# The second layer's products by Strassen's seven-product scheme on blocks of 1024 tokens

## The chip, the cores and the metric

The kernel runs on one core of a Trainium2 chip. TensorE (PE) multiplies matrices from SBUF into PSUM, VectorE (DVE) and ScalarE (ACT) work elementwise, SyncE (SP) issues DMAs between DRAM and SBUF; GpSimd (POOL) is all but unused here. The metric is the device time of one execution in microseconds (us), median of several runs. Each engine executes its own instructions in a fixed order, and waits by semaphores for the others.

## The reference

Chunked attention with memory keys, then two feed-forward layers without bias, on 3072 tokens of width 512, all in float32:

```python
# attention: 4 batches, 8 heads, 768 positions, width 64; chunks of 32 see 8 memory keys + 56 neighbours
x = attention(q, k, v, mem_k, mem_v).transpose(0, 2, 1, 3).reshape(3072, 512)
h = x @ w_in                                   # layer one: 512 x 2048
g = np.maximum(h, 0.0) + np.log1p(np.exp(-np.abs(h)))
y = g @ w_out                                  # 2048 x 512
h2 = y @ w2_in                                 # layer two: 512 x 2048
out = (h2 - np.tanh(h2)) @ w2_out              # 2048 x 512
```

## The kernel before

**Precision.** TensorE multiplies operands of a shorter float (F32R). Every float32 operand is therefore kept as a high and a low part, and a product is three matmuls: high by high, high by low, low by high (`mm3`, lines 285 to 287 of before). Weights arrive as 64-bit floats, are rebuilt as float32 (`split_w`, lines 127 to 131) and split into the two parts (138, 140).

**Work.** The 3072 tokens go in six blocks of 512 (`j`). For each block and each of 16 slices of the hidden width (`f`), `ff_h` makes 128 hidden features x 512 tokens (4 slices of the width, so 12 matmuls of 128x128 by 128x512) in one of two PSUM banks `ps_h`; `chain1` (layer one) or `chain2` (layer two) applies the nonlinearity and splits the result into `gh`, `gl`; two `f` later (`LAG`), `run_y` adds its share to four output banks `ps_y`, 12 matmuls more. So a block is 16 x 24 = 384 matmuls in either layer, and layer two is 6 x 384 = 2304. In layer two `ff_y2` takes `gh`, `gl` as the stationary side, so its result is token-major and leaves by `out2`. Between the layers `out1` splits each result bank (354, 355) and stores it to DRAM (`x2d`), and `load_x2` brings a block of it back.

**Attention** runs for the first block in an opening whose order is written out by hand (`OPENING`), about the first 120 us; afterwards, during block `j` of layer one, for block `j+1`: a unit of 128 tokens at a time, in pieces between the matmuls (`at_do`): scores (line 186), softmax (DVE 206, 210, 223 to 226, ACT 220), transposes (231) two `f` after the scores, values (250), and the split into `x` (262, 264).

**Order.** PE's order is that of the code. The other engines' order is made by a list scheduler before the run, which takes what is ready, the urgent first: `hp(HPC)` lifts the chains, `hp(HPA)` attention, and `hp(HPW)` puts the splitting of layer two's weights last; it takes place in layer one's last block and layer two's first one. At run time each engine, SP's queue of DMA issues too, goes strictly in that order, and whoever waits holds up what is behind. Tiles come from pools with a fixed number of buffers (`gpool` 3, `opool` 4), and a new tile waits until an old one's last reader, or the DMA that stores it, is done.

Of the kernel before, what the change touches and what calls it, by code (L numbers as in the profile page):

```python
# [8 lines left out]
F32 = mybir.dt.float32  # L9
# [11 lines left out]
P = 128  # L21
# [38 lines left out]
HPA = 60  # L60
HPW = -80
EXP_BIAS = 2.0 ** -112
# [3 lines left out]
def attention_ffn_ffn(  # L66
# [18 lines left out]
    opool = ctx.enter_context(tc.tile_pool(name="o", bufs=4))  # L85
    apool = ctx.enter_context(tc.tile_pool(name="a", bufs=2))
    dpool = ctx.enter_context(tc.tile_pool(name="d", bufs=1, space=bass.MemoryType.DRAM))
# [34 lines left out]
    def split_w(raw, f, kinds="io", t=None):  # L122
        n = len(kinds)
        lo, hi = raw[:, :, :, 0], raw[:, :, :, 1]
        c = opool.tile([P, n, 512], U32, name="o")
        w = c.bitcast(F32)
        nc.scalar.mul(w, hi.bitcast(F32), EXP_BIAS)
        yield
        nc.vector.tensor_scalar(out=c, in0=c, scalar1=3, scalar2=None, op0=ALU.logical_shift_left)  # L129
        for src, k, op in ((hi, 0x80000000, ALU.bitwise_and), (lo, 29, ALU.logical_shift_right)):  # L130
            nc.vector.scalar_tensor_tensor(  # L131
                out=c, in0=src, scalar=k, in1=c, op0=op, op1=ALU.bitwise_or
            )
        yield
        if t is None:
            t = wpool.tile([P, n, 2, 512], F32R, name=f"w{f}")
        h, l = t[:, :, 0, :], t[:, :, 1, :]
        nc.scalar.copy(out=h, in_=w)
        yield
        nc.vector.tensor_tensor(out=l, in0=w, in1=h.bitcast(F32), op=ALU.subtract)  # L140
        for i, kind in enumerate(kinds):
            weights[kind, f] = h[:, i], l[:, i]

    def run(steps):
# [138 lines left out]

    def mm3(ps, ah, al, bh, bl, first, last):
        nc.tensor.matmul(out=ps, lhsT=ah, rhs=bh, start=first, stop=False)  # L285
        nc.tensor.matmul(out=ps, lhsT=ah, rhs=bl, start=False, stop=False)  # L286
        nc.tensor.matmul(out=ps, lhsT=al, rhs=bh, start=False, stop=last)  # L287

# [29 lines left out]

    def chain2(key, ps):
        t = tpool.tile([P, N], F32, name="t")  # L320
        nc.scalar.activation(out=t, in_=ps, func=AF.Tanh)  # L321
        nc.vector.tensor_tensor(out=t, in0=ps, in1=t, op=ALU.subtract)  # L322
        run(split_g(key, t, nc.vector))

    def split_g(key, t, hi_eng):
# [16 lines left out]

    def ff_y2(key, f):
        gh, gl = gt.pop(key)
        wh, wl = weights["o", f]
        for e in range(UB):
            c = slice(e * P, (e + 1) * P)
            mm3(ps_y[e], gh[:, c], gl[:, c], wh, wl, f == 0, f == NF - 1)

    def out1(j):  # L350
        for e in range(KT):
            o = opool.tile([P, 2, N], F32R, name="o")
            src = ps_y[e][:, :N]
            nc.scalar.copy(out=o[:, 0, :], in_=src)
            nc.vector.tensor_tensor(
                out=o[:, 1, :], in0=src, in1=o[:, 0, :].bitcast(F32), op=ALU.subtract
            )
            nc.sync.dma_start(out=x2d[j][:, e], in_=o.bitcast(F32))

    def out2(j):  # L360
        for e in range(UB):
            t0 = j * N + e * P
            o = opool.tile([P, DM], F32, name="o")
            if t0 == NTOK - P:
                nc.vector.tensor_copy(out=o[:, : DM // 2], in_=ps_y[e][:, : DM // 2])
                nc.scalar.copy(out=o[:, DM // 2 :], in_=ps_y[e][:, DM // 2 :])
            elif e % 2:
                nc.vector.tensor_copy(out=o, in_=ps_y[e])
            else:
                nc.scalar.copy(out=o, in_=ps_y[e])  # L370
            nc.sync.dma_start(out=out[t0 : t0 + P, :], in_=o)

    def load_x2(j):
        x = x_tile(NB + j)
        nc.sync.dma_start(out=x.bitcast(F32), in_=x2d[j])

    class Weights:
# [6 lines left out]

        def run(self, count):
            while self.at < min(count, NF):
                self.load(self.at + 1)
                run(split_w(*self.staged.pop(0)))
                self.at += 1

    nc.scalar.preload_act_table_set("natural_log_exp_and_others")
    nc.vector.memset(zeros, 0.0)
    make_identity(nc, ident)

    w1, w2 = Weights(w1i, w1o), Weights(w2i, w2o)

# [3 lines left out]
    def run_y():  # L400
        layer, j, f = pend.pop(0)
        if layer == 1:
            ff_y1((1, j, f), f)
            if f == NF - 1:
                with hp(HPC):
                    out1(j)
        else:
            ff_y2((2, j, f), f)
            if f == NF - 1:
                with hp(HPC):  # L410
                    out2(j)

    with tc.manual_schedule(engines={mybir.EngineType.PE}):
# [68 lines left out]

        pend = [(1, 0, NF - LAG + i) for i in range(LAG)]
        for j in range(1, NB):
# [18 lines left out]
            for f in range(NF):  # L503
                ps = ff_h(f, slot, x)
                with hp(HPC):
                    run(chain1((1, j, f), ps, nc.vector))
                piece(2 * f)
                pend.append((1, j, f))
                if len(pend) > LAG:
                    run_y()  # L510
                piece(2 * f + 1)
                slot += 1
                if j == NB - 1 and f >= LAG:
                    with hp(HPW):
                        w2.load(f - LAG + 1)
                        w2.run((f - LAG) * 3 // 4)


        load_x2(0)
        for j in range(NB):  # L520
            x = x_tile(NB + j)
            for f in range(NF):
                if j == 0:
                    with hp(HPW):
                        w2.load(f + 15)
                        w2.run((NF - 1 - LAG) * 3 // 4 + 1 + f * 7 // 10)
                ps = ff_h(f, slot, x)
                with hp(HPC):
                    chain2((2, j, f), ps)
                pend.append((2, j, f))  # L530
                if len(pend) > LAG:
                    run_y()
                slot += 1
                if f == 2 and j + 1 < NB:
                    load_x2(j + 1)
        while pend:
            run_y()

# [4 lines left out]
def _layout(q, k, v, mem_k, mem_v, moe_w_in, moe_w_out, moe2_w_in, moe2_w_out):  # L543
# [47 lines left out]
```

## Time and profile before

| | |
|---|---|
| timed runs | 1138.92, 1138.95, 1139.1 us (median 1138.95) |
| span of the profiled execution | 1136.8 us; the profile gives no other time for that execution |
| PE busy / DVE busy / ACT busy | 1118.9 / 567.6 / 380.7 us |
| granted clock of TensorE | full (2.4 GHz) in every slice |
| DMA | 97.63 MB, mean 86 GB/s |

The span runs from the first instruction to the last. "Busy" of PE counts overlapped matmuls once; a matmul's own duration (about 390 ns) is longer than its pitch, the time from one start to the next, since it drains while the next one streams. The waits name who was waited for. PE's clock was full throughout, so times of one stage can be compared with those of another.

### The profile page before, as it was taken

What the parts mean: (1) busy time and instruction counts of PE and PEld (TensorE: products, weight loads), DVE (VectorE), ACT (ScalarE), POOL (GpSimd) and SP (SyncE); (2) the same over time, 40 slices, a digit from 0 to 9 for tenths busy, and PEclk for the clock granted to TensorE, in tenths of its full rate; (3) what the DMA queues carried; (4) which work ended last, traced back from release to release, by engine and by line L of the source; (5) the groups of instructions that cost most, each with busy time, mean ns of one, the idle gap of its engine ahead of it and who ended that gap; (6) DMA issues with size and microseconds to landing.
All of it is one profiled execution on the core that took longest, in us unless ns stands there. A gap on an engine that the chain in (4) does not pass through costs nothing.

```text
span 1136.8 us, 18028 instructions
## 1 busy us (share of the span) xinstructions
PE 1118.9 (98%) x7781; PEld 918.8 (81%) x7781; DVE 567.6 (50%) x899; ACT 380.7 (33%) x667; POOL 0.7 (0%) x6
## 2 busy tenths in 40 slices
PE   6999999999999999999999999999999999999998
PEld 5678888888888888888888888888888888888887
DVE  6999543454444445444996933333333333333332
ACT  5897533343343334334765311111111111111111
POOL 0000000000000000000000000000000000000000
PEclk9999999999999999999999999999999999999999
DMA  9952221131131123004558003003003002000001
GB/s 379 409 187 65 76 93 48 66 132 65 47 121 47 48 78 137 20 1 185 188 197 319 1 1 111 1 1 111 1 1 112 1 1 102 11 1 10 28 1 38
DMA packets 23984, 97.63 MB, mean 86 GB/s; under 512 B 2656, under 2 KB 2656, under 8 KB 23136
## 3 DMA queue, kind: packets, MB, share of 16 engines
q1 hardware_dynamic: 23904, 96.48, 23.1%
q8 instruction: 61, 1.00, 0.4%
q14 instruction: 19, 0.16, 0.0%
HBM read 77.59 MB, written 18.87 MB: 85 GB/s over the span
## 4 chain that ended last, share of the span: by engine, by line
PE 90%; DVE 6%; ACT 2%; issue 1%; DMA 0%; ACTq 0%
PE ps_y L285 15%; PE ps_y L287 14%; PE ps_y L286 14%; PE ps_h L285 14%; PE ps_h L287 14%; PE ps_h L286 14%; DVE o L131 2%; PE ps_a L250 2%; PE ps_a L186 1%; DVE w L140 1%; DVE o L129 1%; PE ps_a L231 1%; DVE t L313 1%; DVE gl L333 0%; ACT sm L215 0%
## 5 line engine op out<-in xcount | busy, mean ns | idle before, releaser
L287 PE MATMUL ps_h<-x,w 128*128 128x512 f32 x764 | 297.7, 390 | 1.7 <-DVE w L140 1.6
L285 PE MATMUL ps_h<-x,w 128*128 128x512 f32 x764 | 298.1, 390 | 0.5 <-DVE t L313 0.5
L286 PE MATMUL ps_h<-x,w 128*128 128x512 f32 x764 | 297.4, 389 | 0.0
L322 DVE TENSOR_TENSOR t<-ps_h,t 128x512 f32<-128x512 f32 x96 | 66.3, 691 | 298.2 <-ACT t L321 298.2
L321 ACT ACTIVATE t<-ps_h 128x512 f32<-128x512 f32 x96 | 57.5, 599 | 419.4 <-PE ps_h L287 419.4
L287 PEld LDWEIGHTS ps_h<-x,w 128*128 128x128 f32 x764 | 143.4, 188 | 32.5 <-DVE w L140 2.6
L285 PEld LDWEIGHTS ps_h<-x,w 128*128 128x128 f32 x764 | 143.5, 188 | 31.0 <-DVE t L313 1.1
L286 PEld LDWEIGHTS ps_h<-x,w 128*128 128x128 f32 x764 | 143.3, 188 | 29.5
L313 DVE SCALAR_TENSOR_TENSOR t<-ps_h,t 128x512 f32<-128x512 f32 x96 | 66.0, 688 | 188.9 <-ACT t L311 188.8
L285 PE MATMUL ps_y<-gh,w 128*128 128x512 f32 x384 | 154.2, 402 | 0.0
L286 PE MATMUL ps_y<-gl,w 128*128 128x512 f32 x384 | 150.1, 391 | 1.2 <-DVE gl L333 1.2
L287 PE MATMUL ps_y<-gh,w 128*128 128x512 f32 x384 | 150.2, 391 | 0.0
L287 PE MATMUL ps_y<-w,gl 128*128 128x512 f32 x384 | 149.4, 389 | 0.0
L285 PE MATMUL ps_y<-w,gh 128*128 128x512 f32 x384 | 149.4, 389 | 0.0
L286 PE MATMUL ps_y<-w,gh 128*128 128x512 f32 x384 | 149.4, 389 | 0.0
L333 DVE TENSOR_TENSOR gl<-t,gh 128x512 fp32r<-128x512 f32 x192 | 132.4, 690 | 12.3 <-ACT gh L329 1.4
L309 ACT ACTIVATE t<-ps_h 128x512 f32<-128x512 f32 x96 | 57.5, 599 | 214.3 <-PE ps_h L287 213.9
L286 PEld LDWEIGHTS ps_y<-gl,w 128*128 128x128 f32 x384 | 72.2, 188 | 16.5 <-DVE gl L333 2.6
L287 PEld LDWEIGHTS ps_y<-gh,w 128*128 128x128 f32 x384 | 72.1, 188 | 15.7
L285 PEld LDWEIGHTS ps_y<-gh,w 128*128 128x128 f32 x384 | 72.1, 188 | 15.5
L286 PEld LDWEIGHTS ps_y<-w,gh 128*128 128x128 f32 x384 | 72.1, 188 | 15.0
L285 PEld LDWEIGHTS ps_y<-w,gh 128*128 128x128 f32 x384 | 72.0, 188 | 15.0
(66 smaller groups left out, 820.4 us busy)
## 6 DMA issues: line engine op xcount, KB each, us to landing
qk<-in_qk SPq DMA_DIRECT2D x22, 768.0 KB, 6.2
x2d<-o SPq DMA_DIRECT2D x24, 512.0 KB, 3.1
x<-x2d SPq DMA_DIRECT2D x6, 2048.0 KB, 7.8
v<-in_vv SPq DMA_DIRECT2D x22, 512.0 KB, 3.6
w<-in_w1i SPq DMA_DIRECT2D x16, 512.0 KB, 10.6
w<-in_w1o SPq DMA_DIRECT2D x16, 512.0 KB, 10.7
w<-in_w2i SPq DMA_DIRECT2D x16, 512.0 KB, 3.7
w<-in_w2o SPq DMA_DIRECT2D x16, 512.0 KB, 4.7
```

The lines of the kernel that those rows point to most:

```text
L129: nc.vector.tensor_scalar(out=c, in0=c, scalar1=3, scalar2=None, op0=ALU.logical_shift_left)
L131: nc.vector.scalar_tensor_tensor(out=c, in0=src, scalar=k, in1=c, op0=op, op1=ALU.bitwise_or)
L140: nc.vector.tensor_tensor(out=l, in0=w, in1=h.bitcast(F32), op=ALU.subtract)
L250: nc.tensor.matmul(out=ps[h : h + 64, p % 2, 2 * P + t0 : 2 * P + t0 + CHUNK], lhsT=a["v"][r, c, p, :], rhs=a["pT"][r, p, CHUNK * c : CHUN ...
L285: nc.tensor.matmul(out=ps, lhsT=ah, rhs=bh, start=first, stop=False)
L286: nc.tensor.matmul(out=ps, lhsT=ah, rhs=bl, start=False, stop=False)
L287: nc.tensor.matmul(out=ps, lhsT=al, rhs=bh, start=False, stop=last)
L309: nc.scalar.activation(out=t, in_=ps, func=AF.Abs)
L313: nc.vector.scalar_tensor_tensor(out=t, in0=ps, scalar=0.0, in1=t, op0=ALU.max, op1=ALU.add)
L321: nc.scalar.activation(out=t, in_=ps, func=AF.Tanh)
L322: nc.vector.tensor_tensor(out=t, in0=ps, in1=t, op=ALU.subtract)
L333: nc.vector.tensor_tensor(out=gl, in0=t, in1=gh.bitcast(F32), op=ALU.subtract)
```

## The change

Layer one is as it was, up to `out1`, which now stores its four banks as plain float32 (`y1d`), two copied by ACT and two by DVE. Layer two takes blocks of 1024 tokens (`b`, three of them). Each of its two matrix products is seen as a 2 x 2 by 2 x 2 product of blocks and made from seven block products instead of eight, with sums of blocks on both sides and of the results.

- **Weight sums (`job_w`)**: 16 jobs in layer one, one per four `f` from block 1 on. Each loads a 64-bit weight slice, rebuilds it, forms 7 blocks of 256 columns, splits them and stores them to DRAM (`wid`, `wod`), by 6 stores.
- **Token sums (`job_x`)**: six jobs, four in layer one, two in layer two's second block, each with four differences, seven splits and seven stores (`x2d`).
- **`h_phase(b)`**: 8 slices `p` of hidden rows, two at a time in turn, each with seven products of 6 matmuls, one to each of the two PSUM banks of its pair in turn. The partial results 1, 6 and 5 are copied by ACT (`kept`), 2, 7 and 3 are added by DVE (`summed`), and four results go through tanh into `g2`.
- **`y_phase(b)`**: seven products of 8 slices, each slice 6 matmuls with weights stationary (so the result is feature-major). Before each slice ACT makes `gh` and DVE makes `gl`; three of the seven also need one DVE subtraction each.
- **Weights from DRAM (`Ring`)**: five buffers of 1 MB; whenever one is used up, the next load is issued.
- Layer one's weight slices 7 and 15 now share a buffer, and are reloaded from DRAM in each block (`load_w1`).

The matmuls of layer two per block of 1024 tokens are 8 x 7 x 6 in `h_phase` and 7 x 8 x 6 in `y_phase`, 672 in all.

```diff
-HPW = -80
+HPJ = -120
+PRODUCTS = (1, 2, 6, 5, 7, 3, 4)
+SHARED = (7, 15)
...
     def out1(j):
         for e in range(KT):
+            o = opool.tile([P, N], F32, name="o")
+            if e % 2:
+                nc.vector.tensor_copy(out=o, in_=ps_y[e][:, :N])
+            else:
+                nc.scalar.copy(out=o, in_=ps_y[e][:, :N])
+            nc.sync.dma_start(out=y1d[j // 2][e % 2][:, j % 2, e // 2], in_=o)
+
+    def split_to(src, dst, shape):
...
+        nc.scalar.copy(out=hi, in_=src)
+        nc.vector.tensor_tensor(out=lo, in0=src, in1=hi.bitcast(F32), op=ALU.subtract)
+        for s, t in ((0, hi), (1, lo)):
+            for at, n, place in dst(s):
+                nc.sync.dma_start(out=place, in_=t[:, at : at + n].bitcast(F32))
+
+    def job_w(kind, p):
...
+        c = opool.tile([P, 4 * HALF], U32, name="o")
+        nc.scalar.mul(c.bitcast(F32), hi.bitcast(F32), EXP_BIAS)
+        nc.vector.tensor_scalar(out=c, in0=c, scalar1=3, scalar2=None, op0=ALU.logical_shift_left)
+        for of, k, op in ((hi, 0x80000000, ALU.bitwise_and), (lo, 29, ALU.logical_shift_right)):
...
+        split_to(w[:, 1:4], lambda s: ((0, 2, place(s, 0, 2)), (2, 1, place(s, 6, 1))), [3, HALF])
+        add, sub = ALU.add, ALU.subtract
+        nc.vector.tensor_tensor(out=w[:, 0], in0=w[:, 0], in1=w[:, 3], op=add)
+        nc.vector.tensor_tensor(out=w[:, 1], in0=w[:, 0], in1=w[:, 1], op=sub)
+        nc.vector.tensor_tensor(out=w[:, 2], in0=w[:, 2], in1=w[:, 1], op=sub)
+        nc.vector.tensor_tensor(out=w[:, 3], in0=w[:, 3], in1=w[:, 1], op=sub)
+        split_to(w, lambda s: ((0, 4, place(s, 2, 4)),), [4, HALF])
...
+    def h_phase(b):
+        held = {}
+        for p, i in h_order:
+            q = PRODUCTS[i]
+            b0, b1 = banks[(p + 2 * (b % 2)) % 4]
+            ps = b1 if i % 2 else b0
...
+            for k in range(2):
+                wh, wl = (w[:, s, k * P : (k + 1) * P] for s in range(2))
+                mm3(ps, wh, wl, x[:, k, 0], x[:, k, 1], k == 0 and q in (1, 2, 5), k == 1, q in (6, 7, 3, 4))
+            ring.done()
+            if i == 3 and p in (0, 4) and 0 < b < NT - 1:
+                with hp(HPJ):
+                    run(job_x(b + 1, p // 4))
...
+                if q in (1, 6, 5):
+                    held[p, q] = kept(ps)
+                elif q == 2:
+                    tanh_rest(g[:, 0], summed(ps, held.pop((p, 1))))
...
+    def y_phase(b):
...
+        for i, q in enumerate(PRODUCTS):
+            ps = [banks[(2 * b + d) % 4][i % 2] for d in range(2)]
+            for p in range(NP):
...
+                nc.scalar.copy(out=gh, in_=src)
+                minus(gl, src, gh.bitcast(F32))
+                if q == 1:
+                    minus(t, g[:, 3], g[:, 1])
+                elif q == 6:
+                    minus(g[:, 0], t, g[:, 0])
+                elif q == 5:
+                    minus(g[:, 2], g[:, 2], t)
+                w = ring.get(half_of_y(b, q, p))[:, p % 4]
+                for d in range(2):
+                    wh, wl = (w[:, s, d * P : (d + 1) * P] for s in range(2))
+                    mm3(ps[d], wh, wl, gh, gl, p == 0 and q in (1, 2, 5), p == NP - 1, q in (6, 7, 3, 4))
+                ring.done()
+                if p == NP // 2 and b + 1 < NT:
+                    x2_load(b + 1, q)
...
-        load_x2(0)
-        for j in range(NB):
...
+        for b in range(NT):
+            h_phase(b)
+            y_phase(b)
```

The first place is PE in layer two, in the middle of a block. Before, the last rows of an output step and the first of a hidden step (`ps_h`, `ps_y` are PSUM banks, `x` the block's tokens, `w` the weights):

```order
L287 MATMUL ps_y2_654<-w8_5694,gl_6589 128x512
L285 MATMUL ps_y3_655<-w8_5694,gh_6588 128x512
L286 MATMUL ps_y3_655<-w8_5694,gh_6588 128x512
L287 MATMUL ps_y3_655<-w8_5694,gl_6589 128x512
L285 MATMUL ps_h1_82<-x1_5866,w11_5873 128x512
L286 MATMUL ps_h1_82<-x1_5866,w11_5873 128x512
L287 MATMUL ps_h1_82<-x1_5866,w11_5873 128x512
L285 MATMUL ps_h1_82<-x1_5866,w11_5873 128x512
```

After, the first products of `h_phase(0)` (`w0`, `w1` and so on hold the token sums of products 1, 2, 6, 5; `x0` is a ring buffer of weights; x6 stands for six matmuls in a row):

```order
L309 MATMUL ps_b0_5569<-w0_5655,x0_3857 128x512 x6
L309 MATMUL ps_h0_81<-w0_5655,x0_3857 128x512 x6
L309 MATMUL ps_b1_5570<-w1_5715,x0_3857 128x512 x6
L309 MATMUL ps_h1_82<-w1_5715,x0_3857 128x512 x6
L309 MATMUL ps_b0_5569<-w2_5750,x0_3857 128x512 x6
L309 MATMUL ps_h0_81<-w2_5750,x0_3857 128x512 x6
L309 MATMUL ps_b1_5570<-w3_5785,x0_3857 128x512 x6
L309 MATMUL ps_h1_82<-w3_5785,x0_3857 128x512 x6
```

Twelve matmuls to a bank have become six, and each bank comes up again after three other groups.

The second place is DVE in layer one, one attention unit. Before (`st` and `sm` belong to the softmax, `t`, `gh`, `gl` to `chain1`):

```order
L264 TENSOR_TENSOR x0_1818<-ps_a_83,x0_1818 128x2x2x128
L206 TENSOR_REDUCE st_1821<-ps_a_83 128x8
L210 TENSOR_TENSOR sm_1822<-ps_a_83,st_1821 128x2x4x64
L223 TENSOR_REDUCE st_1821<-sm_1822 128x8
L224 TENSOR_SCALAR st_1821<-st_1821 128x8
L225 RECIPROCAL st_1821<-st_1821 128x8
L226 TENSOR_TENSOR sm_1822<-sm_1822,st_1821 128x2x4x64
L313 SCALAR_TENSOR_TENSOR t_1858<-ps_h1_82,t_1858 128x512
L331 CAST gh_1863<-t_1858 128x512
L333 TENSOR_TENSOR gl_1864<-t_1858,gh_1863 128x512
```

After, another unit, where the rows of a weight job (`o`, line 375 the subtraction of a split, 388 and 390 the rebuilding) stand among those of the softmax and the chain:

```order
L229 TENSOR_REDUCE st_1879<-ps_a_86 128x8
L352 TENSOR_TENSOR gl_1809<-t_1803,gh_1808 128x512
L233 TENSOR_TENSOR sm_1880<-ps_a_86,st_1879 128x2x4x64
L375 TENSOR_TENSOR o_1786<-o_1768,o_1785 128x1024
L246 TENSOR_REDUCE st_1879<-sm_1880 128x8
L247 TENSOR_SCALAR st_1879<-st_1879 128x8
L248 RECIPROCAL st_1879<-st_1879 128x8
L249 TENSOR_TENSOR sm_1880<-sm_1880,st_1879 128x2x4x64
L388 TENSOR_SCALAR o_2011<-o_2011 128x1024
L390 SCALAR_TENSOR_TENSOR o_2011<-w15_2009,o_2011 128x1024
L338 SCALAR_TENSOR_TENSOR t_1916<-ps_h1_82,t_1916 128x512
```

A job's subtraction of 1024 elements now stands between two steps of the softmax.

The third place is DVE in `y_phase(0)`, where product 2 ends and product 6 begins (`o` is an output tile, line 594 the addition that empties a bank; `gl_7005`, `gl_7016`, `gl_7027` are for slices 0, 1 and 2 of product 6):

```order
L520 TENSOR_TENSOR gl_6988<-w14_6691,gh_6987 128x512
L520 TENSOR_TENSOR w7_6262<-w7_6262,w5_6816 128x512
L520 TENSOR_TENSOR w8_6271<-w8_6271,w5_6816 128x512
L520 TENSOR_TENSOR gl_7005<-w5_6816,gh_7004 128x512
L520 TENSOR_TENSOR w9_6402<-w9_6402,w5_6816 128x512
L594 TENSOR_TENSOR o_6998<-ps_b1_5570,kept_6910 128x512
L594 TENSOR_TENSOR o_7001<-ps_h1_82,kept_6912 128x512
L520 TENSOR_TENSOR gl_7016<-w5_6816,gh_7015 128x512
L520 TENSOR_TENSOR gl_7027<-w5_6816,gh_7026 128x512
L520 TENSOR_TENSOR gl_7038<-w5_6816,gh_7037 128x512
```

Both additions, which wait for the last matmul of product 2, stand ahead of the low part for product 6's second slice.

## Rows read from the trace of the kernel before

**Rows 1.** Page, part 1: engine, busy us (share of span), instructions.

```profile
PE 1118.9 (98%) x7781; PEld 918.8 (81%) x7781; DVE 567.6 (50%) x899; ACT 380.7 (33%) x667; POOL 0.7 (0%) x6
```

**Rows 2.** Windows: us from start, busy us (count) by engine, clock, DMA share, GB/s.

```profile
28.00:60.00 32.00, 29.01 (x243) 21.81 (x242) 31.03 (x40) 28.44 (x64) 0.00 (x0) 1.00 1.03 409
212.00:304.00 92.00, 92.00 (x889) 75.49 (x888) 41.93 (x75) 35.17 (x60) 0.00 (x0) 1.00 0.21 73
580.00:600.00 20.00, 20.00 (x90) 16.57 (x89) 19.31 (x25) 13.46 (x18) 0.00 (x0) 1.00 0.54 200
786.00:874.00 88.00, 88.00 (x390) 72.89 (x389) 30.09 (x50) 10.76 (x18) 0.00 (x0) 1.00 0.10 36
```

**Rows 3.** Timeline of SP, layer two: start us, us, issue.

```profile
689.60 0.33 SPq L375 DMA_DIRECT2D x<-x2d  x1
...
950.72 0.33 SPq L375 DMA_DIRECT2D x<-x2d  x1
```

**Rows 4.** Waits, 120 to 1137 us: total us, times, longest us.

```profile
ACT t L321 <- PE ps_h L287: 419.4, 91, 4.8
...
PEld ps_a L250 <- issue: 5.6, 16, 0.4
```

**Rows 5.** Groups by line and shape: count, busy us, mean ns, idle before.

```profile
L285 PE MATMUL ps_h<-x,w 128*128 128x512 f32 x764 | 298.1, 390 | 0.5 <-DVE t L313 0.5
...
L333 DVE TENSOR_TENSOR gl<-t,gh 128x512 fp32r<-128x512 f32 x192 | 132.4, 690 | 12.3 <-ACT gh L329 1.4 <-DVE gh L331 0.5
L131 DVE SCALAR_TENSOR_TENSOR o<-w,o 128x1024 uint32<-128x1024 uint32 x62 | 75.6, 1220 | 1.2
...
L321 ACT ACTIVATE t<-ps_h 128x512 f32<-128x512 f32 x96 | 57.5, 599 | 419.4 <-PE ps_h L287 419.4
L140 DVE TENSOR_TENSOR w<-o,w 128x1024 fp32r<-128x1024 f32 x31 | 37.7, 1218 | 1.0 <-ACT w L138 0.9
L127 ACT ACTIVATE o<-w 128x1024 f32<-128x1024 f32 x31 | 35.3, 1149 | 7.2 <-DMA w<-in_w2o 3.6 <-DVE w L140 2.7 <-ACT x L262 0.4
L138 ACT CAST w<-o 128x1024 fp32r<-128x1024 f32 x31 | 32.6, 1052 | 32.1 <-DVE o L131 31.9
...
L129 DVE TENSOR_SCALAR o<-o 128x1024 uint32<-128x1024 uint32 x31 | 21.2, 684 | 1.0 <-ACT o L127 1.0
...
L355 DVE TENSOR_TENSOR o<-ps_y,o 128x512 fp32r<-128x512 f32 x24 | 16.3, 683 | 12.1 <-ACT o L354 12.1
...
L365 DVE COPY o<-ps_y 128x256 f32<-128x256 f32 x1 | 0.4, 423 | 0.7 <-PE ps_y L287 0.7
```

**Rows 6.** Timeline of DVE: start us, us, instructions that don't wait.

```profile
574.56 0.68 DVE L129 TENSOR_SCALAR o<-o 128x1024 uint32<-128x1024 uint32 x1
...
575.16 0.68 DVE L333 TENSOR_TENSOR gl<-t,gh 128x512 fp32r<-128x512 f32 x1
...
575.77 1.21 DVE L140 TENSOR_TENSOR w<-o,w 128x1024 fp32r<-128x1024 f32 x1
```

**Rows 7.** Timeline: one attention unit, scores, softmax's last step, transposes.

```profile
154.61 0.86 PE L186 MATMUL ps_a<-qk 64*32 64x64 f32 x64
...
161.34 0.69 DVE L226 TENSOR_TENSOR sm<-sm,st 128x512 f32<-128x512 f32 x1
...
166.44 0.60 PE L231 MATMUL ps_a<-ident,sm 128*128 128x128 f32 x4
```

**Rows 8.** DMA issues: count, KB each, median us to landing; queue's packets first.

```profile
q1 hardware_dynamic: 23904, 96.48, 23.1%
...
x<-x2d SPq DMA_DIRECT2D x6, 2048.0 KB, 7.8
...
w<-in_w1i SPq DMA_DIRECT2D x16, 512.0 KB, 10.6
```

**Rows 9.** Timeline of the end: last matmul, then the last copies.

```profile
1132.54 0.39 PE L287 MATMUL ps_y<-w,gl 128*128 128x512 f32 x1
1132.96 0.42 DVE L365 COPY o<-ps_y 128x256 f32<-128x256 f32 x1 [0.67 <-PE ps_y L287]
```

More of the change, by code (lines that the diff above doesn't have):

```diff
@@ L142, in split_w, with load_w1 @@
             weights[kind, f] = h[:, i], l[:, i]
+        weights["slot", f] = t
+    def load_w1(f):
+        t = wpool.tile([P, 2, 2, 512], F32R, name=f"w{SHARED[0]}")
+        nc.sync.dma_start(out=t.bitcast(F32), in_=w1d[f])
+        for i, kind in enumerate("io"):
+            weights[kind, f] = t[:, i, 0, :], t[:, i, 1, :]
     def run(steps):
@@ L281, in at_do, with mm3 @@
                 run(x_out(u))
[L284 to L287, printed above, removed]
+    def mm3(ps, ah, al, bh, bl, first, last, on=False):
+        for i, (a, b) in enumerate(((ah, bh), (ah, bl), (al, bh))):
+            nc.tensor.matmul(
+                out=ps, lhsT=a, rhs=b, start=first and i == 0, stop=last and i == 2,
+                skip_group_check=on,
+            )
     gt = {}
@@ L317, in chain1 @@
         yield from split_g(key, t, hi_eng)
[L319 to L323, printed above, removed]
     def split_g(key, t, hi_eng):
@@ L357, in out1 @@
             )
[L358 to L371, printed above, removed]
@@ L377, in attention_ffn_ffn @@
+        minus(b21, b21, b22)
+        put(4, b21)
     class Weights:
@@ L400, in run_y, with work @@
     def run_y():
[L401 to L411, printed above, removed]
+        j, f = pend.pop(0)
+        ff_y1((1, j, f), f)
+        if f == NF - 1:
+            with hp(HPC):
+                out1(j)
+    jobs = [("i", p) for p in range(NP)] + [(0, e) for e in range(2)]
+    jobs += [("o", p) for p in range(NP)] + [(1, e) for e in range(2)]
+    jobs = [job_w(*x) if isinstance(x[0], str) else job_x(*x) for x in jobs]
+    def work():
+        if jobs:
+            with hp(HPJ):
+                for _ in jobs.pop(0):
+                    pass
     with tc.manual_schedule(engines={mybir.EngineType.PE}):
@@ L480, in attention_ffn_ffn @@
                     next(going[kind, i], None)
-        pend = [(1, 0, NF - LAG + i) for i in range(LAG)]
+        for f in SHARED:
+            raw = weights["slot", f]
+            nc.sync.dma_start(out=w1d[f], in_=raw.bitcast(F32))
+        pend = [(0, NF - LAG + i) for i in range(LAG)]
         for j in range(1, NB):
@@ L512, in attention_ffn_ffn @@
                 slot += 1
[L513 to L516, printed above, removed]
-        load_x2(0)
-        for j in range(NB):
[L521 to L535, printed above, removed]
+                if f == SHARED[0] + LAG:
+                    load_w1(SHARED[1])
+                elif f == LAG - 1 and j > 1:
+                    load_w1(SHARED[0])
@@ L536, in attention_ffn_ffn @@
         while pend:
             run_y()
+        for t in slots[3:]:
+            ring.add(t)
+        banks = [ps_b, tuple(ps_h), tuple(ps_y[:2]), tuple(ps_y[2:])]
+        for b in range(NT):
+            h_phase(b)
+            y_phase(b)
 _INS = ["qk", "vv", "w1i", "w1o", "w2i", "w2o"]
```

208 lines of the change are left out of this document (184 added, 24 removed).

## The prediction

> **What bounds the kernel now.** I read the page's engine line first: PE is busy 1118.9 of 1136.8 us [rows 1]. Busy alone can deceive with pipelined matmuls, so next the windows: from 212 us on PE fills every stretch to the last hundredth, at full clock, while DVE, ACT and the DMA engines are far from full [rows 2]. The waits after the opening say the same from the other side: ACT waits 419.4 us for PE, and the largest PE wait is 5.6 us in 16 pieces of at most 0.4, for its own issue [rows 4]. So in layer two the end is set by the number of matmuls times their pitch. The pitch I take from the loads of layer two's blocks, issued at the same place of each block: three blocks from 689.60 to 950.72, so 87.04 us for 384 matmuls, 0.2267 us each [rows 3]. A matmul's own 390 ns [rows 5] is longer because it drains under the next one.
>
> **What the change removes.** Layer two has 6 x 384 = 2304 matmuls of 128x128 by 128x512 before and 3 x 672 = 2016 after, of the same shape and with as many weight loads each. 288 fewer at 0.2267 are 65.3 us. All lie on the path that sets the end, since PE has no gaps there. The removed weight splitting, chains and second `out1` pass lay beside PE and give nothing.
>
> Here a rule speaks against the size of this. The row says 0.2267 us per matmul in a stream of 2304 of them [rows 3]. The Trainium skill (TensorE: Matmul & The Clock Gate, Back-to-back issue gap) gives about 131 ns for a sustained stream with 512 columns; by that 288 matmuls would be worth only 37.7 us. The trace disagrees for these operands, and the sum goes by the row.
>
> **What it adds on PE: waits for DVE at product borders.** In `y_phase`, where product 2 ends, DVE's order has both additions that empty its banks ahead of the low part for product 6's second slice. Let S be the end of product 2's last matmul's slot. At the end of the kernel DVE starts 0.19 us after such a slot (1132.54 + 0.23, then 1132.96) [rows 9]. DVE operations of 512 columns last 0.69 but follow each other every 0.60 when they don't wait (574.56, 575.16, 575.77) [rows 6]. So the additions start at S+0.19 and S+0.79, the low part at S+1.39 and ends at S+2.08. PE wants it for the eighth matmul, at S + 7 x 0.2267 = S+1.59. That is 0.5 us, in each of three blocks: 1.5 us. At the other borders two slices stand ahead of the additions or copies, and the same working gives S+2.1 behind DVE's additions and S+2.7 behind ACT's copies, against S+2.95: no wait, but behind ACT only 0.2 us to spare. Inside the three products with two DVE operations a slice, DVE needs 1.2 us per slice and PE 6 x 0.2267 = 1.36; it keeps up. The upper bound for these borders is that all 18 inside the products cost 0.5 each, 9 us.
>
> In `h_phase` a bank comes up again after three other groups of six matmuls, 4.1 us. The copy or addition that must come between takes 0.6 or 0.7 us [rows 5], so it may be 3 us late. A pair of slices (14 groups, 19.0 us) asks of DVE 16 operations at 0.60, 9.6 us, and of ACT 14, 8.4 us. I put this at nothing: the three groups between hide it.
>
> **What it adds in layer one.** A weight job on DVE, from [rows 5]: 0.68 + 2 x 1.22 for the rebuilding, 1.22 and about 0.95 (an estimate between the rows for 512 and 1024 columns) for the low parts, 4 x 0.42 for the sums (the nearest row is a copy of 256 columns): 7.0 us. Four jobs a block are 28 us; `out1` has two DVE operations of 0.68 where it had four. DVE goes from 42 to 68 of 92 us [rows 2]. ACT gets 1.15 + 1.05 + about 0.8 per job, and goes from 35 to 46. In a stretch with DVE at 19.3 of 20 us PE still had no gap [rows 2]; that stretch had no attention, though. What attention needs: scores end at 155.47, softmax ends at 162.03, the transposes start at 166.44, on time [rows 7]. So each of 16 units has 4.4 us to spare, three or four job operations of 1.22 in its way. Lower bound nothing; upper bound one operation too many for each, 16 x 1.22 = 20 us. I take 1.0, near the lower end, since the order has the jobs mostly ahead of or behind a softmax and the trace with DVE at 97% shows no wait.
>
> The jobs store 16 x 7 x 2 x 128 = 28,672 pieces of 1 KB, 29.4 MB. The queue's 23,904 packets of 4 KB in the mean took 23.1% of 16 engines' span [rows 8], 0.18 us each. If a piece of 1 KB costs as much as a packet of 4 KB, that is 315 us of all engines; if it goes by bytes, 80. Layer one after the opening lasts some 470 us with a DMA share of 0.21 [rows 2]; so the share rises to 0.4 or, at worst, 0.9. I take the lower end, as bytes and time go together in the stretch that is full (409 GB/s at a share of 1.03). The Trainium skill (DMA: Bandwidth & Descriptors, Specifications) puts the smallest transfer at line rate at 512 bytes, which would mean the lower end; no run here shows it.
>
> **What it adds in DMA of layer two.** Per block 14.7 MB of weights for each phase, 7.3 MB of token sums (for two of the three), 2.1 MB out, and once 9.4 MB for the two late jobs: 118.5 MB in 2016 x 0.2267 = 457 us, 259 GB/s. The opening moved 409 [rows 2]. The tightest refill in `h_phase` is asked for when the seventh group of a pair ends and is needed eight groups later, 10.9 us; in `y_phase` four slots of 5.4 us lie between. A load of 2 MB alone landed in 7.8 us [rows 8], these are of 1 MB or less. So hidden; if that cover is gone, see the third rival. The late jobs bring DVE in that `h_phase` from 38 to 52 of 76 us (2 x 11 operations of 0.60 more); I give them 0.5 us.
>
> **End and sum.** The last bank's copy is now one of 512 columns instead of two halves side by side: +0.2 us. Span: 1136.8 - 65.3 + 1.5 + 1.0 + 0.5 + 0.2 = 1074.7. The runs' median, 1138.95, is 2.15 above the span, which I take to lie around it and to stay: 1076.9, so 1077. Without any wait it would be 1136.8 - 65.3 + 2.15 = 1073.7, and nothing removed goes below that.
>
> **Rivals.**
> 1. *The gain is eaten by engines that go in order.* The softmax units in layer one pay their 20 us and the borders of `y_phase` their 9 instead of 2.5 together: 1077 + 26 = 1103 at the most, about 1090 in the middle. For it: only 0.2 us to spare at the borders with ACT's copies, and jobs that wait for a landing DMA in front of a chain. Against it: PE's waits of 0.4 at most so far [rows 4], and 4.4 us to spare in attention [rows 7].
> 2. *The pitch is not what a matmul is worth.* By the 131 ns the gain is 37.7 us and the time 1077 + 27.6 = 1105. Against it is the row itself.
> 3. *The ring starves, and it is slower than before.* If a refill lands more than 10.9 us after its issue, `h_phase` stops once per pair, about 12 times in all, and everything behind waits. The price is 12 x (landing - 10.9); at 16 us of landing the gain is gone, at 17 the time is 1077 + 73 = 1150. For it: in the opening, with the DMA engines full, loads of 512 KB took 10.6 us [rows 8]. Against it: the demand is 63% of what moved then, and loads are issued one at a time as buffers come free.
> 4. *It doesn't do what it says*, were matmuls of layer two not fewer: excluded, as the order has 2016.
>
> **Chances.** Forecast, with its own spread 1074 to 1082: 0.80. Rival 1: 0.15; rival 2: 0.01; rival 3: 0.03; something not thought of on the slow side: 0.01. The range goes from 1073.5 (no wait at all) to 1090, the middle of rival 1; beyond it lie half of rival 1 and the rest, about 0.12. A difference under 0.2% (2.3 us) can't be told from none. Faster: the first two rivals and the forecast, 0.96; slower: rival 3, 0.03; the same: 0.01.
>
> **What would show it.** Right: PE busy to the last hundredth in windows of layer two, 2016 matmuls there at 0.2267; layer two's outputs about 152.4 us apart from block to block; waits of PE for `gl` about 0.5 us three times; DVE near 70 of 92 us in layer one without PE waits on `sm` or `gl`; ring loads landing within 10 us. Wrong: PE waiting on ring buffers or `w` by DMA (third rival), on `sm`, `pT` or `gl` over 10 us in total (first), or a pitch other than 0.2267 while the weights come from DRAM.

## The result and the profile after

The changed kernel takes 1081.67 us in the median (four runs, 1078.88 to 1085.63), the kernel before beside it 1138.93. The ratio is 0.950, interval 0.948 to 0.952. The forecast was 1077, with 1074 to 1082 as its own spread and 1073.5 to 1090 as the range. The profiled execution took 1079.7 us, with a span of 1077.9.

Page of the changed kernel, engines [rows 1]:

```profile
PE 1055.5 (98%) x7493; PEld 864.0 (80%) x7493; DVE 744.6 (69%) x1186; ACT 556.8 (52%) x961; POOL 0.7 (0%) x6
```

PE has 7493 matmuls for 7781, the 288 fewer. Next the windows of the changed kernel, four of layer one and two of layer two (columns as in [rows 2]):

```profile
120.00:212.00 92.00, 92.00 (x827) 75.25 (x827) 62.33 (x104) 45.27 (x70) 0.00 (x0) 1.00 0.65 210
212.00:304.00 92.00, 89.82 (x817) 73.42 (x817) 66.24 (x112) 45.79 (x72) 0.00 (x0) 1.00 0.66 215
304.00:396.00 92.00, 92.00 (x844) 75.60 (x837) 60.09 (x106) 44.94 (x76) 0.00 (x0) 1.00 0.61 216
396.00:488.00 92.00, 91.05 (x882) 74.36 (x880) 69.97 (x117) 46.53 (x72) 0.00 (x0) 1.00 0.70 224
...
640.00:790.00 150.00, 149.88 (x662) 123.62 (x661) 101.83 (x160) 74.22 (x125) 0.00 (x0) 1.00 0.76 269
790.00:942.00 152.00, 151.89 (x670) 125.31 (x669) 103.38 (x163) 75.26 (x126) 0.00 (x0) 1.00 0.83 295
```

Layer two is full. Layer one has a hole of 2.2 us in its second window and the beginning of another in the fourth. The waits of PE, and then of its weight loads, say where (first stretch 120 to 1078 us, second 612 to 1078):

```profile
PE ps_a L254 <- DVE sm L249: 3.8, 2, 2.2
```

```profile
PEld ps_b L309 <- DVE gl L520: 1.5, 4, 0.5
PEld ps_y L309 <- DVE gl L520: 0.7, 2, 0.5
```

The first line is attention: the transposes wait for the softmax, twice, for 2.2 and 1.6 us. The other two are the product borders of `y_phase`. What they cost in all is read from the ends of layer two, its first and its last matmul (PE's timeline, changed kernel):

```profile
615.39 1.52 PE L309 MATMUL ps_b<-w,x 128*128 128x512 f32 x6
...
1073.57 0.39 PE L309 MATMUL ps_h<-gh,x 128*128 128x512 f32 x1
```

1073.57 + 0.23 - 615.39 = 458.4 us, and 2016 x 0.2267 = 457.0, so 1.4 us of waits. Layer one is compared at the scores of its last attention unit, before and after:

```profile
496.27 0.86 PE L186 MATMUL ps_a<-qk 64*32 64x64 f32 x64
```

```profile
501.16 0.86 PE L209 MATMUL ps_a<-qk 64*32 64x64 f32 x64
```

That is 4.9 us later, of which 0.5 stood there already at 97 us, in the opening (the same scores start at 97.02 before and 97.57 after; in the traces of the experiments below with the same opening, between 96.26 and 97.61). So the profiled execution closes: 1136.8 - 65.3 + 0.5 + 4.4 (layer one) + 1.4 (borders) + 0.1 (end) = 1077.9.

### The profile page after: what moved, and what is told of

The parts are those of the page before. It is cut to its first block, busy times and chain, and to the rows that moved or that the text cites. A ratio compares the mean times of both kernels' runs of the same rounds, so it can differ in the third digit from the quotient of the medians.

```text
span 1077.9 us, 18703 instructions
## 1 busy us (share of the span) xinstructions
PE 1055.5 (98%) x7493; PEld 864.0 (80%) x7493; DVE 744.6 (69%) x1186; ACT 556.8 (52%) x961; POOL 0.7 (0%) x6
## 4 chain that ended last, share of the span: by engine, by line
PE 71%; DVE 16%; DMA 7%; ACT 3%; issue 2%; SPq 0%; DVEq 0%; ACTq 0%
PE ps_y L309 32%; PE ps_h L309 26%; PE ps_b L309 10%; DVE w L520 4%; DVE gl L520 2%; DMA w<-in_w1i 2%; DVE o L147 2%; PE ps_a L273 1%; DVE o L390 1%; DMA wid<-o 1%; DVE t L338 1%; DMA qk<-in_qk 1%; DVE w L156 1%; DMA wod<-o 1%; PE ps_a L209 1%
## 5 line engine op out<-in xcount | busy, mean ns | idle before, releaser
L309 PE MATMUL ps_h<-x,w 128*128 128x512 f32 x1140 | 275.5, 390 | 2.3 <-DVE w L156 1.8
L309 PEld LDWEIGHTS ps_h<-x,w 128*128 128x128 f32 x1140 | 213.1, 188 | 48.7 <-DVE w L156 2.6
L569 ACT CAST gh<-w 128x512 fp32r<-128x512 f32 x168 | 104.7, 624 | 106.2 <-DVE gl L520 66.2
L520 DVE TENSOR_TENSOR gl<-w,gh 128x512 fp32r<-128x512 f32 x168 | 115.1, 689 | 60.0 <-ACT gh L569 59.4
L309 PE MATMUL ps_y<-w,x 128*128 128x512 f32 x402 | 94.2, 389 | 0.0
L309 PEld LDWEIGHTS ps_y<-w,x 128*128 128x128 f32 x402 | 75.5, 188 | 15.7
L309 PE MATMUL ps_h<-gh,x 128*128 128x512 f32 x176 | 68.5, 389 | 0.0
L309 PE MATMUL ps_b<-gh,x 128*128 128x512 f32 x176 | 68.5, 389 | 0.0
L352 DVE TENSOR_TENSOR gl<-t,gh 128x512 fp32r<-128x512 f32 x96 | 66.0, 689 | 3.1 <-ACT gh L348 1.4
L335 ACT ACTIVATE t<-t 128x512 f32<-128x512 f32 x96 | 60.9, 634 | 2.4
L336 ACT ACTIVATE t<-t 128x512 f32<-128x512 f32 x96 | 60.6, 631 | 2.4
```

The source lines that it names most:

```text
L309: nc.tensor.matmul(out=ps, lhsT=a, rhs=b, start=first and i == 0, stop=last and i == 2, skip_group_check=on,)
L335: nc.scalar.activation(out=t, in_=t, func=AF.Exp, scale=-1.0)
L336: nc.scalar.activation(out=t, in_=t, func=AF.Ln, bias=1.0)
L352: nc.vector.tensor_tensor(out=gl, in0=t, in1=gh.bitcast(F32), op=ALU.subtract)
L520: nc.vector.tensor_tensor(out=out, in0=x, in1=y, op=ALU.subtract)
L569: nc.scalar.copy(out=gh, in_=src)
```

## What the experiments showed

Each kernel was timed beside the kernel before. Theories and rivals have letters (A, A2, C2 and so on) of their own; the text on record ahead of each measurement is what was expected.

**The changed kernel again.** No edit.

> The changed kernel once more, to see where its executions differ (1078.9 to 1085.6 us so far, while the kernel before keeps to 0.6 us). The mean granted clock of an execution fell with its time: 0.994 at 1085.6, 0.996 at 1083.6, 1.0 at 1079.7. Theory A: layer one has two PE waits for the softmax (2.2 and 1.6 us in the traced execution); in some executions one is longer and the granted clock falls behind it for some 13 us, which costs half of that. Then a trace of a long execution shows the low clock between 290 and 510 us, right behind a PE wait on sm. Rival C: the clock falls in layer two, where PE, DMA and both other engines are busy together, without a wait ahead of it. Then the low clock stands after 615 us. Both: time = 1079.5 plus (1 - clock) x span within 1 us.

The six executions took 1077.65, 1077.73, 1078.54, 1079.58, 1082.51, 1088.05 (median 1079.06), and the kernel before, eleven times beside it, 1138.45 to 1140.12. The mean clock is no guide: the expected sum gives 1086.0 us for the execution of 1082.51 (0.994) and 1084.9 for that of 1088.05 (0.995), the kernel before ran at 0.998 without loss, and e4 below had its shortest time at 0.996. The trace was of the shortest execution, with no low clock after the opening, so it tells nothing between A and C. It had 2.7 us of waits on `sm`.

**Five tiles `o`.**

```diff
-    opool = ctx.enter_context(tc.tile_pool(name="o", bufs=4))
+    opool = ctx.enter_context(tc.tile_pool(name="o", bufs=5))
```

> The pool of the tiles o has five buffers instead of four (the zeros of the opening's filler matmuls are made smaller for it). Theory A: the job's last low part stands in DVE's queue until the stores of the job's first high part have landed, because it gets that tile's buffer, and the softmax behind it is late; with a fifth buffer it waits for nothing. PE's two waits on sm (3.8 us together, and 0.3 more) go, the span falls from 1077.9 to about 1073.8, the time to about 1075.6, and all executions keep a clock of 1.0. Rival B: DVE is simply too full beside the attention, the buffer has nothing to do with it: the waits on sm stay at 3 to 5 us and the time at 1079 to 1085.

It took 1080.31 to 1080.82, in the median 1080.55. Theory A's sum fell: the waits on `sm` grew to 4.6 us in four pieces. But the executions lay within 0.5 us. How a wait arises is seen in the changed kernel's own trace, around its first unit that is late (timeline, 277 to 292 us):

```profile
277.44 0.86 PE L209 MATMUL ps_a<-qk 64*32 64x64 f32 x64
...
280.02 1.15 ACT L387 ACTIVATE o<-w 128x1024 f32<-128x1024 f32 x1 [3.18 <-DMA wid<-o]
...
281.94 1.23 DVE L390 SCALAR_TENSOR_TENSOR o<-w,o 128x1024 uint32<-128x1024 uint32 x1
...
282.90 0.57 ACT L285 CAST x<-ps_a 128x512 fp32r<-128x512 f32 x1
...
283.68 1.22 DVE L390 SCALAR_TENSOR_TENSOR o<-w,o 128x1024 uint32<-128x1024 uint32 x1
...
286.35 0.68 DVE L229 TENSOR_REDUCE st<-ps_a 128x8 f32<-128x512 f32 x1
...
290.77 0.69 DVE L249 TENSOR_TENSOR sm<-sm,st 128x512 f32<-128x512 f32 x1
...
291.61 0.63 PE L254 MATMUL ps_a<-ident,sm 128*128 128x128 f32 x4 [2.18 <-DVE sm L249]
```

The scores end at 278.3. ACT's next operation is the first of the *next* job, and it stands 3.18 us for a tile `o` that is still being stored. Behind it in ACT's order are the chain and the copy of the previous unit's attention output, and the softmax starts at 286.35, 8 us after its scores. The arithmetic has its part in that: from 281.21 on DVE is never idle, and 3.1 us of its work ahead of the softmax are the next job's rebuilding (0.69 at line 388 and the two rows of line 390). The softmax ends 13.2 us after its scores, where it ended 6.6 us after them before [rows 7]; of the 6.6 us more, 4.4 were to spare, and 2.2 are the stop. Five tiles only move ACT's wait. In e2 the same operation in the same place:

```profile
280.86 1.12 ACT L387 ACTIVATE o<-w 128x1024 f32<-128x1024 f32 x1 [2.80 <-DMA wid<-o]
```

**No weight jobs; jobs without their stores.** These two price the jobs in layer one. In both, layer two reads other weights from DRAM, as many bytes.

```diff
-    jobs = [job_w(*x) if isinstance(x[0], str) else job_x(*x) for x in jobs]
+    jobs = [iter(()) if isinstance(x[0], str) else job_x(*x) for x in jobs]
```

```diff
-        for s, t in ((0, hi), (1, lo)):
-            for at, n, place in dst(s):
-                nc.sync.dma_start(out=place, in_=t[:, at : at + n].bitcast(F32))
```

> Layer one without the sixteen weight jobs (left out: the making of the weight sums; layer two reads as many bytes of layer-one weights from DRAM instead, so that its products are of other numbers). It prices the jobs in layer one as a whole. Theory A and rival B: no PE wait on sm after the opening, span 1077.9 - 4.1 = 1073.8, time 1075.6; what e2 does not reach of that is DVE's load and not the buffer. If the low clock of some executions comes from the stalls of layer one, all executions here have a clock of 1.0; if it comes from layer two (rival C), the spread of some 6 us stays.

> The weight jobs with all their arithmetic but without their stores (left out: the stores of the weight sums; layer two reads as many bytes of layer-one weights instead). After e2 theory A stands as A2: it is not the one buffer but the landing of stores. Jobs follow each other every two hidden slices, so ACT's first operation of the next job waits for a tile o whose store is still under way (3.2 us in the changed kernel, 2.8 with five buffers), and the copies, the chain and the softmax behind it in ACT's queue are late. By A2 no PE wait on sm is left: span 1073.4 as in e3, time 1075.1, no spread above 1 us. Rival B: the arithmetic of the jobs in DVE's and ACT's order makes the softmax late, stores or not: the waits on sm stay at 2.7 to 4.6 us, time about 1079.

Without the jobs the time is 1075.13 (1073.93 to 1075.18), the span 1073.4. With their arithmetic but no stores the time is 1076.57 (1076.49 to 1077.58), the span 1074.8. PE has no waits on `sm` after the opening in the first; in the second it has

```profile
PE ps_a L254 <- DVE sm L249: 1.7, 2, 1.3
```

So neither theory had it alone. Against e1's median of 1079.06 the jobs cost 3.9 us: 1.4 by their arithmetic (rival B) and 2.5 by their stores (A2). The 2.5 is not firm, as the changed kernel's own two medians lie 2.6 us apart; but all ten of its executions (1077.65 or more) are above all four without stores (1077.58 or less). Nor is it shown to be the landing alone, since the stores' traffic goes with it. In either kernel the executions lie within 1.3 us of each other; that speaks against rival C, which put the spread into layer two. The windows of 120 to 580 us give the price of the stores in DMA, the changed kernel first, then e5:

```profile
120.00:580.00 460.00, 456.23 (x3936) 374.20 (x3936) 309.69 (x521) 222.50 (x351) 0.00 (x0) 1.00 0.65 217
```

```profile
120.00:580.00 460.00, 458.29 (x3947) 376.19 (x3946) 315.15 (x532) 226.81 (x359) 0.00 (x0) 1.00 0.47 162
```

That is (0.65 - 0.47) x 460 = 83 us of all 16 engines, for (217 - 162) x 460 us, or 25.3 MB.

**The kernel before with 288 matmuls fewer.**

```diff
-            mm3(ps_y[e], gh[:, c], gl[:, c], wh, wl, f == 0, f == NF - 1)
+            mm3(ps_y[e], gh[:, c], gl[:, c], wh, wl, f == 0, f == NF - 1, e > 0)   # e > 0: two products of three
```

> The kernel before with 288 matmuls fewer in layer two and nothing else changed (left out: the product of the low part of g with the high weights in three of four row tiles of y). Forecast's step: a matmul is worth its pitch, 0.2267 us, so 1138.95 - 65.3 = 1073.7 within 1 us. By 131 ns a matmul: 1101. If something beside PE (DVE's splitting of weights, the chain between the two products) is next in line, the time lies between 1073.7 and 1101 and PE shows waits in layer two.

It took 1074.14 (1073.4 to 1074.45) beside 1139.15: 65.0 us less, 0.2257 us a matmul. So the matmuls left out are worth the whole gain forecast for the changed scheme, and in the kernel before nothing else was in line behind PE.

**Jobs four slices apart.** After e2 and e5 the remedy seemed to be distance. A copy of one column ties each job to its slice:

```diff
+        nc.vector.tensor_copy(out=raw.bitcast(F32)[:, 0, :1], in_=tie[0].bitcast(F32)[:, :1])
...
+                    tie[:] = gt[1, j, f][1:]
                     work()
```

> The full computation. Each weight job is tied to its slice by a copy of one column, so that jobs follow each other every four hidden slices (21.8 us) instead of in bursts of four, two slices apart (10.9 us), and the tiles o have five buffers. A2: every store has landed by the time its buffer is wanted, so PE's waits on sm fall under 1 us, the span to about 1073.8 and the time to 1075.5, all executions within 1 us. Rival B: the same operations stand between the softmax steps, in other units: 3 to 5 us of waits on sm, time about 1079.

> As e6, with four buffers. Only the wait of a job's own last low part for its first part's stores is left, 1.4 to 3.2 us on DVE a job; ACT's waits for stores go. A2: a wait of 3 us on DVE fits into the 4.4 us that attention has to spare, so PE waits at most 1 us on sm, time 1075.5 to 1076.5. If DVE's wait was the heavier half: 2 to 3 us on sm, time about 1078. Rival B: about 1079.

Both failed, by 29 and 35 us against e1: 1108.11 (1104.53 to 1108.69) with five tiles, 1113.90 (1111.39 to 1116.13) with four. The waits on `sm` are gone, as A2 had it, though the job operations still stand among the softmax's. A wait that no theory had is there instead. PE's waits, e6 and then e7, from 110 us on:

```profile
PE ps_y L309 <- ACT o L368: 20.1, 4, 7.4
```

```profile
PE ps_y L309 <- ACT o L368: 27.6, 4, 9.2
```

L368 is `out1`, which empties `ps_y` at a block's end into tiles `o` too. The job of the block's last slice now stands right ahead of it on ACT, and the next block's first product has no bank. At the first of the four, the changed kernel's copy, and then e7's timeline:

```profile
236.50 0.57 ACT L368 COPY o<-ps_y 128x512 f32<-128x512 f32 x1
```

```profile
240.36 0.60 PE L254 MATMUL ps_a<-ident,sm 128*128 128x128 f32 x4
...
245.86 0.59 ACT L368 COPY o<-ps_y 128x512 f32<-128x512 f32 x1 [2.23 <-DMA wid<-o]
...
246.50 0.79 PE L309 MATMUL ps_y<-gh,w 128*128 128x512 f32 x1 [5.54 <-ACT o L368]
```

A tile that is still being stored is the smaller part of it: 2.2 of the 5.5 us here. For the rest the copy stands behind both splits of the job and the next slice's chain. In e6 the first copies of the four blocks wait 2.1 us in all for stores, of 20.1 us that PE stops, and at the longest stop (7.4 us) the copy waits for nothing. With four tiles stores weigh more: ahead of e7's second and third copy DVE's last low part waits 1.8 and 3.3 us for them. In e6's longest stop the copy only comes behind the job's last split, which waits for DVE's sums (e6, ACT):

```profile
557.87 1.04 ACT L374 CAST o<-o 128x1024 fp32r<-128x1024 f32 x1 [3.03 <-DVE o L404]
558.83 0.58 ACT L368 COPY o<-ps_y 128x512 f32<-128x512 f32 x1
```

So what costs most is the place of the whole job ahead of the copy in ACT's order. Why the scheduler puts the copy there is not shown; the job and the copy take tiles from the same pool.

The first stop in e7 is 5.5 us, but the kernel loses more. The windows of e7 behind it:

```profile
246.50:248.50 2.00, 2.00 (x5) 1.61 (x6) 1.17 (x2) 0.59 (x1) 0.00 (x0) 0.50 0.74 249
248.50:250.50 2.00, 2.00 (x6) 1.52 (x5) 0.69 (x1) 0.00 (x0) 0.00 (x0) 0.50 1.06 348
250.50:252.50 2.00, 2.00 (x6) 1.60 (x5) 0.00 (x0) 0.00 (x0) 0.00 (x0) 0.51 0.73 194
252.50:254.50 2.00, 2.00 (x10) 1.62 (x10) 0.00 (x0) 0.00 (x0) 0.00 (x0) 1.00 0.00 0
```

The granted clock is 0.50, the lower of the two levels (1.2 GHz), for 6 us after the stop, with 5 or 6 matmuls started in 2 us where there are 10 at full clock. By these counts that is about 3 us more, an estimate. It closes: 27.6 us of stops and four times 3 us make 39.6, and e7's span of 1113.0 us is 38.9 above the changed kernel's without its waits on `sm`. In the changed kernel's trace stops of 1.6 and 2.2 us left the clock at 1.00 (the first windows above).

**Additions behind the low parts.** In DVE's order at the border of products 2 and 6:

```diff
-            with hp(HPC):
+            with hp(HPY if q == 2 else HPC):    # HPY = -40
```

> The changed kernel, with the additions that empty the banks of product 2 put behind the low parts for product 6's first slices in DVE's order (one addition after each). Forecast's step: the wait there was 0.46 us in each of three blocks; it goes, and layer two from its first to its last matmul lasts 457.0 us instead of 458.4. The time falls by 1.4, within the spread of layer one's waits, to about 1077.7 in the median. If the wait comes from the landing weights or the copy on ACT instead of the order on DVE, layer two stays at 458.4.

Layer two came out as expected. PE's first and last matmul there in e8 are

```profile
614.83 1.52 PE L309 MATMUL ps_b<-w,x 128*128 128x512 f32 x6
...
1071.77 0.39 PE L309 MATMUL ps_h<-gh,x 128*128 128x512 f32 x1
```

which is 1071.77 + 0.23 - 614.83 = 457.2 us, 1.2 less. The time shows nothing of it: the median is 1081.54 where 1077.7 was expected, from 1077.9 to 1087.35, as wide as before.

**The last `out1` apart.** The same shortage at the start of layer two, in the changed kernel (timeline of ACT, then of PE):

```profile
617.66 0.59 ACT L368 COPY o<-ps_y 128x512 f32<-128x512 f32 x1 [7.93 <-DMA x2d<-o]
...
620.45 0.59 ACT L368 COPY o<-ps_y 128x512 f32<-128x512 f32 x1 [1.71 <-DMA x2d<-o]
620.93 0.59 ACT L511 COPY kept<-ps_h 128x512 f32<-128x512 f32 x1
```

```profile
622.19 1.52 PE L309 MATMUL ps_h<-w,x 128*128 128x512 f32 x6
```

PE needs the bank at 622.19 that ACT has emptied at 621.52; 0.7 us to spare, behind a store of a token-sum job.

```diff
+            if j == NB - 1:
+                o = lpool.tile([P, N], F32, name="sum" if e % 2 else "kept", bufs=3 if e % 2 else 4)
```

> The changed kernel, with one edit: the last block's out1 writes its four tiles into buffers of layer two's pool and not into tiles o. Theory C2 on the executions that are 4 to 10 us longer: at the start of layer two ACT stands 6.5 to 7.9 us in out1's first copy, because its tile o is still being stored by the last token-sum job; product 1's first copies queue behind it and come 0.7 us before PE needs their bank (621.5 against 622.2). When the store lands some us later, PE stops, and after a stop of 5.5 us the clock was low for some 9 us in e7. Then with this edit all executions lie within 1.5 us of each other, at 1077.5 to 1079.7, with clocks of 0.998 and more. Rival D: the long executions stall elsewhere (the loads of x2d or of the ring, the softmax): the spread stays 4 to 10 us.

> e8 (the additions behind the low parts) with e9's edit (the last out1 in layer two's pool), so that beside e8, whose executions lay between 1077.9 and 1087.4, only the last out1 differs. Theory C2: the executions above 1081 come from ACT standing in the last out1 at the start of layer two; here all lie between 1075.5 and 1080.5, the rest of the spread being the softmax waits of layer one (2.7 to 5.9 us in the traces so far). Rival D: the long executions stall elsewhere, and one or two of five lie above 1081.5. Layer two from first to last matmul: 457.0 us, as in e8.

e9 took 1080.39, from 1077.38 to 1081.40; e12 took 1080.29, from 1077.08 to 1081.77, and its layer two lasts 457.2 us. The copy that was 0.7 us ahead of PE is 3.3 us ahead of it in e9 (619.4 against 622.7). By what was expected C2 is not borne out: e9's spread is 4.0 us where C2 had 1.5 and rival D 4 to 10, and one of e12's five lies above 1081.5, as D had it. Part of that is the softmax, whose waits alone differ (5.9 us in e9's trace, 3.1 in e12's). The low clock in e7 lasted until 6 us after the stop, not the 9 of the expectation.

For C2 speaks that in ten executions with the edit none is above 1081.8, while of the nineteen without it (the changed kernel, e1, e8 and e11 below) eight are between 1082.5 and 1088.1. But two of the eight are e11's, 1083.34 and 1083.91, and e11's trace does not have the shortage. ACT's order is another one there, and though one of the `out1` copies waits 1.3 us for a store, the copy of product 1's second bank is free of it and waits only for PE:

```profile
618.30 0.59 ACT L511 COPY kept<-ps_h 128x512 f32<-128x512 f32 x1 [0.77 <-PE ps_h L309]
```

PE needs that bank at 622.18, 3.3 us later, as in e9. So C2 may hold for some long executions and does not explain these two. The cause of the spread stays open: no long execution fell to the profiler, so no stop of one was seen.

**Four ring slots for five.**

```diff
-        for t in slots[3:]:
+        for t in slots[3:4]:
```

> The changed kernel with four ring slots for the weights instead of five. It tests the cover that the forecast gave the refills (10.9 us for the tightest, landing in 7 us or less). With four slots one load less is in flight: the tightest refill of h_phase then has about one group, 1.4 us, to the group that needs it, so PE stops some 5 us in each pair of slices, 12 times, and the clock falls behind it: 60 us or more, about 1140 or longer. If the ring has slack to spare, the time stays at 1079 to 1082.

It took 1081.74 (1079.17 to 1083.91), the same as with five. The expectation had counted wrongly: with four slots a refill is asked for at the end of the seventh group and needed after seven more, 9.5 us, not one. Both that and the 10.9 us of five slots are more than a ring load takes in the median (5.1 to 7.1 us in the changed kernel).

**All together.** Last `out1` apart, additions behind low parts, five tiles, and the tie at `f % 4 == 1`, so that a block's last job is two slices ahead of `out1`.

> The full computation with four edits: last out1 apart as in e9, additions behind low parts as in e8, five tiles o, and jobs tied to every fourth slice as in e6 but two slices earlier, so that a block's last job has its stores landed when out1 wants its tiles. A2: no PE wait on sm, none on ps_y's copies in layer one, none on gl in layer two: span 1136.8 - 65.3 + 0.2 = 1071.7 to 1072.5, time 1073.4 to 1074.3. If the wait of out1 only moves, as in e6 and e7, PE shows waits on ps_y of 1 to 8 us a block and the time lies between 1078 and 1105.

It took 1076.30 (1074.34 to 1077.56), a ratio to the kernel before of 0.945, interval 0.944 to 0.946: 2.8 us below e1's median of the changed kernel and 5.4 below its first median. The waits on `sm` and on `ps_y` are gone. It stays 2.6 us above the 1073.7 that the prediction had for no wait at all, and a new one is behind that (PE's waits, 120 to 1076 us):

```profile
PE ps_h L309 <- DVE x L287: 2.9, 2, 1.9
```

The low part of the next block's attention output is late behind a job that now stands there. Ahead of the longer wait, ACT stands for the job's weight slice, a load this time, with the chain and the attention copy behind it:

```profile
320.57 1.15 ACT L391 ACTIVATE o<-w 128x1024 f32<-128x1024 f32 x1 [3.62 <-DMA w<-in_w2i]
```

It wasn't followed further.

## Why the prediction was right, and where it was off

*The gain.* It was 65.3 us by the pitch, and 65.0 measured by itself (e4). The pitch is what a matmul is worth, and rival 2, with 37.7, is out. The Trainium skill (TensorE: Matmul & The Clock Gate, Back-to-back issue gap) has about 131 ns for a sustained matmul with 512 columns, from which the 37.7 was an estimate; e4 measures 225.7 ns for these operands, and the measurement decides.

*The borders of `y_phase`.* 1.5 us were forecast from DVE's order, 1.4 found, and 1.2 of them went when the order was changed (e8). Outputs come 152.8 us apart, which is 152.3 for 672 matmuls and one wait of 0.5; the prediction's 152.4 had left its own wait out (SP's timeline, changed kernel, each block's first stores):

```profile
714.03 0.94 SPq L597 DMA_DIRECT2D out<-o  x2
...
866.84 0.94 SPq L597 DMA_DIRECT2D out<-o  x2
...
1019.63 0.93 SPq L597 DMA_DIRECT2D out<-o  x2
```

*Layer one* is the term that was mis-sized: 1.0 us taken, 4.4 found in the profiled execution, inside the bounds of nothing to 20. Of the 4.4, 3.8 are the two waits on `sm`; in the other traces with the same jobs (e1, e8, e9, e11, e12) these are 2.7 to 5.9. The load itself was right (68 of 92 us forecast for DVE, 60 to 70 found; 46 for ACT, 45 to 47 found), and that load by itself cost 1.4 us (e5 against e3). The step left out is a job's *tiles*. The prediction counted what a job's stores take of the DMA engines, and named jobs that wait for a landing DMA in rival 1 without a price. It did not ask when a tile that is being stored comes free, and who stands behind the instruction that wants it. Waits of the changed kernel, 120 to 1078 us:

```profile
DVE o L375 <- DMA wid<-o: 9.6, 5, 3.0
DVE o L375 <- DMA wod<-o: 8.1, 5, 3.2
...
ACT o L387 <- DMA w<-in_w2i: 5.3, 2, 2.9
...
ACT o L387 <- DMA wid<-o: 3.2, 1, 3.2
...
ACT o L387 <- DMA wod<-o: 3.1, 1, 3.1
...
ACT o L387 <- DMA w<-in_w2o: 2.8, 2, 1.5
```

The same operation of a job waits on ACT for its weight slice as well, 8.1 us in all. So rival 1, in-order engines that eat the gain, was there with 4 of its 26 us. In the unit shown above a landing store and a job's arithmetic made the stop together; by the medians the stores cost more, within the uncertainty said there. e6 and e7 lose more than the 26, 29 and 35 us, when a whole job stands ahead of the copy that frees a bank at a block's end.

*Luck.* The opening came 0.5 us later in the profiled execution, for which the forecast has no term, and this stands against the 0.5 for the late jobs, which was not found.

*DMA.* The stores' price was taken at its lower end, 80 us of all engines, and e5 measures 83 for 25.3 MB; at that rate the 29.4 MB are 96 (an estimate), far from the 315 of the upper end. Ring loads landed, in the median, within the 10 us forecast (DMA issues of the changed kernel: KB each, median us to landing). The late token-sum jobs cost at most 0.2 us for the 0.5 given, as e8's whole layer two is 0.2 us longer than its matmuls.

```profile
x<-wod SPq DMA_DIRECT2D x33, 1024.0 KB, 5.7
...
w<-x2d SPq DMA_DIRECT2D x21, 1024.0 KB, 7.4
...
wid<-o SPq DMA_DIRECT2D x16, 512.0 KB, 5.6
```

Rival 3 had nothing for it, not even with a slot less (e11).

*From one execution to the median.* The prediction took the 2.15 us between span and median as fixed. It is 1.8 in the profiled execution, 1079.7; the other 2.0 us to 1081.67 are the spread of 7 us in four runs, which the kernel before doesn't have (0.7 us). The forecast has no term for a spread between executions, and what makes it is not shown.

## What to carry to other kernels

Work that is hidden beside a full engine has two prices: its operations, and the time for which its output tiles are held until their stores have landed. Count tiles wanted against tiles landed, and look who stands behind the instruction that takes the next one; on an in-order engine that may be the copy that frees a bank of the bounding engine. When a hidden job is moved, look first at what it will stand ahead of on the in-order engines: here distance between jobs cured one wait, and put a job ahead of a copy that PE needed, which cost seven times as much.

## What was not expected of the hardware

A stop of PE can cost more than its length: after 5.5 us without work the clock was granted at the lower level for 6 us, and the next block's first products ran at half pace (e7), while stops of 1.6 and 2.2 us left it at 1.00. And a mean granted clock below 1 need not cost anything: in e9's trace the low clock lay in the opening, 20 to 28 us, and attention units behind it came no later than in the others.
